# Modulation rows of a spectral and gated-MLP block: four of six parts summed as columns and read back through DRAM

## The chip, the cores and the metric

One core of a Trainium2 chip runs the whole kernel in one launch. The metric is device time in microseconds, the median of several executions. A profile is one more execution, recorded by the hardware: it gives the start and duration of every instruction on TensorE (PE), VectorE (DVE), ScalarE (ACT), GpSimd (POOL) and the DMA queues, of which SyncE (SP) issues most. "Span" is the time from the first to the last recorded instruction.

## What is computed

Cut to what matters here (S = 2048 rows, D = 512, all float32):

```python
mod = (silu(c) @ w_mod).reshape(6, 512)        # c: 512 numbers, w_mod: 512 x 3072
sa, ca, ga, sb, cb, gb = mod                   # parts 0..5, one row of 512 each
h = layernorm(x) * (1 + ca) + sa
a, b = h @ dft_hid_re.T, h @ dft_hid_im.T
x = x + ga * (dft_seq_re @ a - dft_seq_im @ b)
h = layernorm(x) * (1 + cb) + sb
z = gelu(h @ w_in); z1, z2 = z[:, :896], layernorm(z[:, 896:])
x = x + gb * ((z1 * (w_sp @ z2 + b_sp)) @ w_out)
```

The case is about `mod`: six rows of 512 numbers, each a product of the vector silu(c) with a 512 x 512 block of w_mod. Parts 2 to 5 (ga, sb, cb, gb) are wanted as tiles in which all 128 partitions hold the same row, since they multiply or are added to row-major tiles.

## The kernel before

Every large product is made exactly enough by splitting each float32 operand into a high part (rounded, on ScalarE) and a low remainder (a subtraction, on VectorE), and by three matmuls for each tile: high x high, high x low, low x high (`matmul3`, lines 95 to 97).

The first stage, where the change lies, multiplies the sequence-DFT matrices with the normalised rows. It goes in numbered steps n = 0 to 127. A step takes one chunk, 128 x 512, of a DFT matrix: its 32 x 32 blocks are transposed on VectorE from a loaded block (`turn_two`, two chunks at a time, line 227), its high part `ah` is made on ScalarE (`prep_hi`, line 256), its low part `al` on VectorE (`prep_lo`, line 263), and `mm_a` runs 12 matmuls with it, against the high and low parts `hh` and `hl` of row tile s (`hi_h` line 424, `lo_h` line 429). There are four buffers for `ah` and three for `al`. `prep(n)` makes `al` of chunk n+2, then on even n the transposes of chunks n+4 and n+5, then `ah` of chunk n+3.

All the other work of the stage is put between these steps by hand: `at(n, f, ...)` notes that f is called after step n, in the order of the calls to `at`, and `run(n)` calls what was noted. An engine runs its instructions in the order in which they were issued, so these numbers fix the order on every engine, and on the DMA queues of SP and POOL too. In the loop a step is `prep(n)`, `mm_a(n)`, `run(n)`.

Among the work placed so:

- The hidden-DFT matrices are turned, weighted and split into `hth` and `htl` (tags ht0 to ht3, and w0 for a row that comes back through DRAM). For the second matrix this ends at step 49.
- `post_y` and `post_h`, from step 55 on, finish rows of the first half: `post_y` multiplies by mods[2] on VectorE, `post_h` multiplies by mods[4] on VectorE and adds mods[3] on GpSimd. `scale_wo`, much later, multiplies by mods[5].
- Parts 0 and 1 of the modulation are made as columns: the block of w_mod is loaded in a form in which VectorE can turn it into tiles with the output index on the partitions (`load_columns`, `weigh_column`: a transpose at line 176, then a product with the row silu(c) at line 328), and ScalarE's accumulator sums each partition (`sum_column`, line 333). Four such columns of 128 make a part.
- Parts 2 to 5 go another way. `load_mod` loads the block with the input index on the partitions (line 291). `sum_mod` adds the four slices, each scaled by its number of silu(c), on VectorE (one operation at line 302, three at line 304). `split_mod` splits the sum (lines 90 and 91), and `spread_mod` lets TensorE add over the partitions and spread the result, with a matrix of ones (lines 355 and 356, one pair of matmuls for each part); `keep_mod` copies it out of PSUM on ScalarE (line 296).

Of the kernel before, what the change touches and what calls it, by code (L numbers as in the profile page):

```python
# [8 lines left out]
F32 = mybir.dt.float32  # L9
F32R = mybir.dt.float32r  # L10
AF = mybir.ActivationFunctionType
ALU = mybir.AluOpType

P = 128
# [5 lines left out]
def fnet_gmlp_kernel(  # L20
# [32 lines left out]
    nc = tc.nc  # L53
    S, D = x.shape[1:]
# [5 lines left out]
    ND = D // P  # L60
# [5 lines left out]
    def pool(name, side="left", bufs=1):  # L66
        return tc.tile_pool(name=name, bufs=bufs, side=side, reuse_waits="tile")
# [3 lines left out]
    cpool = ctx.enter_context(pool("cpool"))  # L71
# [4 lines left out]
    dram = ctx.enter_context(tc.tile_pool(name="dram", bufs=1, space=bass.MemoryType.DRAM))  # L76
    ctx.enter_context(tc.manual_schedule())

    def bank(k, name):
        return psum.tile([P, 512], F32, tag=f"bank{k}", bufs=1, name=name)  # L80
# [7 lines left out]
    def split(hi, lo, src):  # L88

        nc.scalar.activation(hi, src, AF.Copy)  # L90
        nc.vector.tensor_tensor(lo, src, hi.bitcast(F32), op=ALU.subtract)
# [31 lines left out]
    def at(n, f, *a):  # L123
        fill.setdefault(n, []).append((f, a))
# [50 lines left out]
    def squares(dst, block, k):  # L175
        nc.vector.transpose(dst.rearrange("p (b i) -> p b i", i=32), block[:, :, 32 * k:32 * k + 32])
# [90 lines left out]
    htpool = p2.enter_context(pool("htpool", "right"))  # L267
    rows = p2.enter_context(pool("rows", "right"))
# [6 lines left out]
    hpre = hq.enter_context(pool("hpre"))  # L275

    ccol = cpool.tile([P, ND], F32, name="ccol")
# [4 lines left out]
    sc = cpool.tile([P, ND], F32, name="sc")  # L282
    busy = rows.tile([P, D], F32, tag="row", bufs=6, name="busy")
    nc.vector.memset(busy, 1.0)
    wm, mods = {}, {}

    def load_mod(j):
        w = hpre.tile([P, ND, D], F32, tag="hraw", bufs=1, name=f"wm{j}")
        wm[j] = [w[:, k, :] for k in range(ND)]
        for k in range(ND):  # L290
            nc.sync.dma_start(wm[j][k], w_mod[k * P:(k + 1) * P, j * D:(j + 1) * D])

    def keep_mod(j, ps, pl, plus_one):
        if j not in mods:
            mods[j] = pl.tile([P, D], F32, tag="ht0" if j == 3 else f"mod{j}", bufs=1, name=f"mod{j}")
        nc.scalar.activation(mods[j], ps, AF.Copy, bias=1.0 if plus_one else 0.0)

    def sum_mod(j, ks=range(4)):
        w = wm[j]
        for k in ks:  # L300
            if k == 0:
                nc.vector.tensor_scalar(w[0], w[0], sc[:, 0:1], None, op0=ALU.mult)
            else:
                nc.vector.scalar_tensor_tensor(w[0], w[k], sc[:, k:k + 1], w[0], op0=ALU.mult, op1=ALU.add)

    WB, WT = {}, {}
    COL = {j: cpool.tile([P, ND], F32, name=f"col{j}") for j in range(3)}

    def load_row():

        nc.sync.dma_start(ccol, c.rearrange("b (k p) -> p (b k)", p=P))
        WB["c"] = rows.tile([P, D], F32, tag="row", bufs=6, name="crow")
        nc.sync.dma_start(WB["c"], c[0].partition_broadcast(P))

    def silu_row():
        nc.scalar.activation(sc, ccol, AF.Silu)
        nc.scalar.activation(WB["c"], WB["c"], AF.Silu)

    def load_columns(j):
        pl, tag = (hpre, "hraw") if j else (spool, "wb")  # L320
        WB[j] = pl.tile([P, 16, P], F32, tag=tag, bufs=1, name=f"wb{j}")
        load_block(WB[j], quad(w_mod, 0, j))

    def weigh_column(j, k):
        tag, bufs = ("row", 6) if k % 2 else ("y", 1)
        WT[j, k] = rows.tile([P, D], F32, tag=tag, bufs=bufs, name=f"wt{j}_{k}")
        squares(WT[j, k], WB[j], k)
        nc.vector.tensor_tensor(WT[j, k], WT[j, k], WB["c"], op=ALU.mult)

    def sum_column(j, k):  # L330

        w = WT.pop((j, k))
        nc.scalar.activation(w, w, AF.Copy, accum_out=COL[j][:, k:k + 1])

    def scale_columns():
        col = COL[1]
# [6 lines left out]
        for _ in range(n):  # L343
            nc.tensor.matmul(ps, ones, busy, start=True, stop=True)

    def split_mod(j):
        w = wm[j][0]
        wm[j] = [hpre.tile([P, D], F32R, tag=f"ht{1 + i}", bufs=1, name=f"ws{j}_{i}") for i in range(2)]
        split(*wm[j], w)

    def spread_mod(j, k, pl, plus_one):

        ps = bank(k, f"modp{j}")
        hi, lo = wm.pop(j)
        nc.tensor.matmul(ps, ones_r, hi, start=True, stop=False)
        nc.tensor.matmul(ps, ones_r, lo, start=False, stop=True)
        keep_mod(j, ps, pl, plus_one)

    X, XG, LN, NRM, h_hi, h_lo = {}, {}, {}, {}, {}, {}

# [605 lines left out]
    for n, *todo in ((0, (turn_one, 3), (prep_hi, 3), (stats_first, 2), (prep_lo, 3), (turn_one, 4), (prep_hi, 4)),  # L966
                     (1, (norm_first, 2), (hi_h, 2), (prep_lo, 4), (lo_h, 2), (turn_one, 5), (prep_hi, 5)),
                     (2, (stats_first, 3), (prep_lo, 5), (turn_one, 6), (prep_hi, 6)),
                     (3, (norm_first, 3), (hi_h, 3), (prep_lo, 6), (lo_h, 3), (turn_one, 7), (prep_hi, 7), (ones_x, 4), (stats_x, 4)),
                     (4, (ones_x, 5), (ones_x, 6), (prep_lo, 7), (turn_two, 8), (stats_x, 5), (prep_hi, 8), (norm_x, 4), (hi_h, 4), (stats_x, 6)),  # L970
                     (5, (ones_x, 7), (prep_lo, 8), (lo_h, 4), (prep_hi, 9), (norm_x, 5), (hi_h, 5)),
                     (6, (prep_lo, 9), (turn_two, 10), (lo_h, 5), (norm_x, 6), (hi_h, 6), (stats_x, 7)),
                     (7, (norm_x, 7)), (8, (lo_h, 6), (hi_h, 7)), (9, (lo_h, 7))):
        for f, *a in todo:
            at(n, f, *a)
    at(0, load_x, 1, range(2, 4))
    at(2, load_row)
    at(9, silu_row)
    at(4, load_x, 2)
    at(5, load_columns, 1)  # L980
# [4 lines left out]
    for s, n in ((8, 10), (9, 10)):  # L985
        m = n + (s == 9)
# [10 lines left out]
    for j, ns in ((1, (13, 15, 17, 18)), (0, (21, 22, 23, 24))):  # L997
        for k, n in enumerate(ns):
            at(n, weigh_column, j, k)
            at(n + 1, sum_column, j, k)  # L1000
# [6 lines left out]
    ones_r = htpool.tile([P, P], F32R, name="ones_r")  # L1007
    at(24, nc.scalar.activation, ones_r, ones, AF.Copy)
    at(26, change_pools)
    for j, turn, weigh, row, fold, hi in ((0, (25, 26, 27, 28), (29, 29, 30, 30), 26, (34, 34, 35, 36), (38, 35, 36, 37)),  # L1010
# [8 lines left out]
        n = weigh[3] + (3 if j == 0 else 1)  # L1019
# [3 lines left out]
        for k in (1, 2, 3, 0):  # L1023
            at(hi[k], make_ht, j, k)
            at(hi[k] + 1, make_ht_lo, j, k)
    for j, load_at, n, m, k, plus_one in ((2, 41, 49, 50, 7, False), (4, 52, 56, 58, 7, True),
                                          (3, 60, 65, 66, 7, False), (5, 68, 79, 80, 6, False)):
        at(load_at, load_mod, j)
        at(n, sum_mod, j, [0, 1])
        at(m, sum_mod, j, [2, 3])  # L1030
        at(m + 1, split_mod, j)
        at(m + 3, spread_mod, j, k, cpool if j == 5 else htpool, plus_one)
    for t in range(NQ):
        n = 8 * NQ * (t + 1)
        for i in range(4):
            y = N2 - 1 if t == NQ - 1 else (54, 56, 58, 60)[i] if t == 0 else n + (7, 9, 11, 13)[i] if t == 1 else n + 1 + 3 * i
# [32 lines left out]
    w0 = ctx.enter_context(ExitStack())  # L1069
# [14 lines left out]
    for i, u in enumerate((r, g, b) for g in range(2) for b in range(4) for r in range(2)):  # L1084
        n = 85 + 5 * i if i < 8 else N2 + (13, 15, 28, 29, 31, 33, 35, 37)[i - 8]
        m = n + (4 if i < 8 or i > 9 else (9, 13)[i - 8])
# [31 lines left out]
    for i, p in enumerate(PROD):  # L1118
        for k in range(8):
            n = NB[p] + 2 * k  # L1120
# [39 lines left out]
    for f in range(NF):  # L1160
        n = NB[6] + 3 * f
# [66 lines left out]
```

## Time and profile before

| | us |
|---|---|
| median of 3 runs | 946.18 (946.17 to 946.81) |
| the profiled execution | 946.31 |
| its span | 944.5 |
| VectorE: the 16 operations of `sum_mod` | 0.48 each at line 302, 0.75 each at line 304 |
| ScalarE: a copy out of PSUM (`keep_mod`) | 0.60 |
| loads of w_mod for parts 2 to 5 (16 of 256 KB) | 4.7 from issue to landing |

Page rows name a source line, an engine, an operation and the tiles as out<-in. A duration of TensorE is that of one matmul from its start to its modelled end, and matmuls overlap; the distance of two starts is what one costs in a row without gaps. "Idle" in square brackets is the time that the engine sat before an instruction, with what ended it. The granted clock of TensorE is full throughout.

### The profile page before, as it was taken

What the parts mean: (1) busy time and instruction counts of PE and PEld (TensorE: products, weight loads), DVE (VectorE), ACT (ScalarE), POOL (GpSimd) and SP (SyncE); (2) the same over time, 40 slices, a digit from 0 to 9 for tenths busy, and PEclk for the clock granted to TensorE, in tenths of its full rate; (3) what the DMA queues carried; (4) which work ended last, traced back from release to release, by engine and by line L of the source; (5) the groups of instructions that cost most, each with busy time, mean ns of one, the idle gap of its engine ahead of it and who ended that gap; (6) DMA issues with size and microseconds to landing.
All of it is one profiled execution on the core that took longest, in us unless ns stands there. A gap on an engine that the chain in (4) does not pass through costs nothing.

```text
span 944.5 us, 12279 instructions
## 1 busy us (share of the span) xinstructions
PE 937.9 (99%) x4160; PEld 781.1 (83%) x4160; DVE 705.7 (75%) x1045; ACT 386.2 (41%) x663; POOL 171.3 (18%) x327
## 2 busy tenths in 40 slices
PE   8999999999999999999999999999999999999998
PEld 6888888888888888888888999888888888888886
DVE  7799857775576657767978587877788688885872
ACT  3695424232232222322876356553544444331221
POOL 1430000221621145123332265200000000000000
PEclk9999999999999999999999999999999999999999
DMA  9997554576528965996398985555554456733551
GB/s 198 245 226 152 110 129 99 148 177 156 145 78 204 278 202 154 284 275 146 93 339 288 321 269 164 148 112 135 123 134 90 108 116 142 205 104 119 170 183 59
DMA packets 251406, 161.25 MB, mean 171 GB/s; under 512 B 134416, under 2 KB 220688, under 8 KB 251216
## 3 DMA queue, kind: packets, MB, share of 16 engines
q1 hardware_dynamic: 237008, 120.62, 52.5%
q0 software_dynamic: 11984, 39.07, 11.4%
q10 hardware_dynamic: 2352, 0.79, 0.3%
q8 instruction: 32, 0.52, 0.3%
q14 instruction: 30, 0.25, 0.1%
HBM read 123.73 MB, written 36.70 MB: 170 GB/s over the span
## 4 chain that ended last, share of the span: by engine, by line
PE 96%; DMA 1%; SPq 1%; DVE 0%; issue 0%; POOL 0%; ACT 0%; ACTq 0%; DVEq 0%
PE gp L97 11%; PE gp L96 11%; PE gp L95 11%; PE gw L95 10%; PE gw L96 10%; PE gw L97 10%; PE yp L97 3%; PE yp L96 3%; PE yp L95 3%; PE z2p L96 3%; PE z2p L95 3%; PE z2p L97 3%; PE op L97 3%; PE op L95 3%; PE op L96 3%; PE z1p L96 1%
## 5 line engine op out<-in xcount | busy, mean ns | idle before, releaser
L256 ACT ACTIVATE ah<-t 128x512 fp32r<-128x512 f32 x263 | 164.5, 627 | 312.6 <-PE gp L97 181.3
L263 DVE TENSOR_TENSOR al<-t,ah 128x512 fp32r<-128x512 f32 x264 | 180.3, 686 | 137.6 <-PE gp L96 61.6
L97 PE MATMUL gp<-ah,hl 128*128 128x512 f32 x480 | 186.9, 389 | 0.3 <-DVE hl L429 0.3
L95 PE MATMUL gp<-ah,hh 128*128 128x512 f32 x480 | 186.7, 389 | 0.0
L96 PE MATMUL gp<-al,hh 128*128 128x512 f32 x480 | 186.7, 389 | 0.0
L97 PE MATMUL gw<-ah,bl 128*128 128x512 f32 x400 | 155.6, 389 | 0.0
L96 PE MATMUL gw<-al,bh 128*128 128x512 f32 x400 | 155.6, 389 | 0.0
L95 PE MATMUL gw<-ah,bh 128*128 128x512 f32 x400 | 155.6, 389 | 0.0
L97 PEld LDWEIGHTS gp<-ah,hl 128*128 128x128 f32 x480 | 90.1, 188 | 19.3 <-DVE hl L429 0.7
L96 PEld LDWEIGHTS gp<-al,hh 128*128 128x128 f32 x480 | 90.1, 188 | 18.8
L95 PEld LDWEIGHTS gp<-ah,hh 128*128 128x128 f32 x480 | 90.1, 188 | 18.8
L97 PEld LDWEIGHTS gw<-ah,bl 128*128 128x128 f32 x400 | 75.1, 188 | 15.7
L95 PEld LDWEIGHTS gw<-ah,bh 128*128 128x128 f32 x400 | 75.1, 188 | 15.5
L96 PEld LDWEIGHTS gw<-al,bh 128*128 128x128 f32 x400 | 75.1, 188 | 15.5
L227 DVE STREAM_TRANSPOSE t<-stage 128x1024 f32<-128x1024 f32 x62 | 76.8, 1239 | 5.5 <-DMA stage<-in_A_dft_seq_re_dram 5.5
L221 DVE STREAM_TRANSPOSE t<-stage 128x1024 f32<-128x1024 f32 x56 | 69.4, 1240 | 0.1
L772 ACT ACTIVATE bh<-z 128x512 fp32r<-128x512 f32 (+1 forms) x56 | 32.8, 586 | 66.1 <-PE gw L96 66.1
L750 POOL DMA_DIRECT2D s_d<-sj x64 | 35.1, 550 | 105.5 <-DVE sj L742 79.3
L95 PE MATMUL yp<-hth,gh 128*128 128x512 f32 x128 | 49.8, 389 | 0.0
L96 PE MATMUL yp<-htl,gh 128*128 128x512 f32 x128 | 49.8, 389 | 0.0
L97 PE MATMUL yp<-hth,gl 128*128 128x512 f32 x128 | 49.8, 389 | 0.0
L96 PE MATMUL z2p<-wil,ah 128*128 128x448 f32 x128 | 46.7, 365 | 0.0
(206 smaller groups left out, 1439.4 us busy)
## 6 DMA issues: line engine op xcount, KB each, us to landing
sj<-in_B_w_sp_dram SPq DMA_DIRECT2D x32, 512.0 KB, 8.4
s_d<-sj POOLq DMA_DIRECT2D x64, 256.0 KB, 4.3
stage<-s_d SPq DMA_DIRECT2D x128, 128.0 KB, 2.8
stage<-in_A_dft_seq_re_dram SPq DMA_DIRECT2D x60, 256.0 KB, 5.3
stage<-in_A_dft_seq_im_dram SPq DMA_DIRECT2D x60, 256.0 KB, 5.4
stage<-in_B_w_sp_dram SPq DMA_DIRECT2D x96, 128.0 KB, 3.2
stage<-h_d SPq DMA_DIRECT2D x32, 256.0 KB, 7.0
wm<-in_w_mod_dram SPq DMA_DIRECT2D x16, 256.0 KB, 4.7
```

Of the source, the lines that this page charges most:

```text
L95: nc.tensor.matmul(acc, ah, bh, start=first, stop=False, skip_group_check=go_on)
L96: nc.tensor.matmul(acc, ah, bl, start=False, stop=False, skip_group_check=go_on)
L97: nc.tensor.matmul(acc, al, bh, start=False, stop=last, skip_group_check=go_on)
L221: nc.vector.transpose(t.rearrange("p r (b i) -> p r b i", i=32), st[:, :, :, 16 * k:16 * k + 32])
L227: nc.vector.transpose(t.rearrange("p k (b i) -> p k b i", i=32), st[:, :, 32 * k:32 * k + 64].rearrange("p b (k i) -> p k b i", k=2))
L256: nc.scalar.activation(AH[n], source(n), AF.Copy)
L263: nc.vector.tensor_tensor(AL[n], source(n), AH[n].bitcast(F32), op=ALU.subtract)
L750: nc.gpsimd.dma_start(s_d[m, r, g][b * P:(b + 1) * P, :], a)
L772: nc.scalar.activation(BH[p, k][:, :w], b_of(p, k), AF.Copy)
```

## The change

Parts 2 to 5 are made as parts 0 and 1 were: transposed and multiplied on VectorE, four columns to a part, and summed by ScalarE's accumulator into a column of 128 numbers. GpSimd then stores each column into a row of 512 numbers in DRAM (`store_mod`, for part 4 after adding 1), and `read_mod` reads the row back into all 128 partitions. `load_mod`, `sum_mod`, `split_mod`, `spread_mod` and `keep_mod` go, with their eight matmuls, and so do the column load of c and its silu. The columns use the buffers of tags w0 and ht1 to ht3, which the hidden-DFT work has left. The columns of a part are spread over the steps given in the table at the end. Apart from that, `lo_h` of row 6 moves from step 8 to step 7.

```diff
-        nc.sync.dma_start(ccol, c.rearrange("b (k p) -> p (b k)", p=P))
-        WB["c"] = rows.tile([P, D], F32, tag="row", bufs=6, name="crow")
+        WB["c"] = cpool.tile([P, D], F32, tag="mod5", bufs=1, name="crow")
         nc.sync.dma_start(WB["c"], c[0].partition_broadcast(P))
...
-        nc.scalar.activation(sc, ccol, AF.Silu)
         nc.scalar.activation(WB["c"], WB["c"], AF.Silu)
+
+    mod_d = [dram.tile([1, D], F32, name=f"mod_d{j}") for j in range(6)]
...
     def weigh_column(j, k):
-        tag, bufs = ("row", 6) if k % 2 else ("y", 1)
-        WT[j, k] = rows.tile([P, D], F32, tag=tag, bufs=bufs, name=f"wt{j}_{k}")
+        if j > 1:
+            WT[j, k] = hpre.tile([P, D], F32, tag=("w0", "ht1", "ht2", "ht3")[k], bufs=1, name=f"wt{j}_{k}")
+        else:
+            tag, bufs = ("row", 6) if k % 2 else ("y", 1)
+            WT[j, k] = rows.tile([P, D], F32, tag=tag, bufs=bufs, name=f"wt{j}_{k}")
...
         w = WT.pop((j, k))
-        nc.scalar.activation(w, w, AF.Copy, accum_out=COL[j][:, k:k + 1])
+        nc.scalar.activation(w, w, AF.Copy, accum_out=COL[j if j < 2 else j % 2][:, k:k + 1])
...
+    def store_mod(j, k, plus_one):
+
+        col = COL[j % 2][:, k:k + 1]
+        if plus_one:
+            nc.gpsimd.tensor_scalar(col, col, 1.0, 1.0, op0=ALU.add, op1=ALU.mult)
+        nc.gpsimd.dma_start(mod_d[j][0].rearrange("(a k i) -> k a i", a=4, i=32)[k], col)
+
+    def read_mod(j, pl):
+        mods[j] = pl.tile([P, D], F32, tag="ht0" if j == 3 else f"mod{j}", bufs=1, name=f"mod{j}")
+        nc.gpsimd.dma_start(mods[j], mod_d[j][0].partition_broadcast(P))
...
-                     (7, (norm_x, 7)), (8, (lo_h, 6), (hi_h, 7)), (9, (lo_h, 7))):
+                     (7, (lo_h, 6), (norm_x, 7)), (8, (hi_h, 7)), (9, (lo_h, 7))):
...
-    for j, load_at, n, m, k, plus_one in ((2, 41, 49, 50, 7, False), (4, 52, 56, 58, 7, True),
-                                          (3, 60, 65, 66, 7, False), (5, 68, 79, 80, 6, False)):
-        at(load_at, load_mod, j)
-        at(n, sum_mod, j, [0, 1])
-        at(m, sum_mod, j, [2, 3])
-        at(m + 1, split_mod, j)
-        at(m + 3, spread_mod, j, k, cpool if j == 5 else htpool, plus_one)
+    for j, load_at, ns in ((2, 41, (48, 48, 49, 50)), (4, 51, (54, 56, 58, 60)),
+                           (3, 61, (64, 65, 66, 67)), (5, 68, (73, 75, 77, 79))):
+        at(load_at, load_columns, j)
+        for k, n in enumerate(ns):
+            at(n, weigh_column, j, k)
+            at(n + 1, sum_column, j, k)
+            at(n + 1, store_mod, j, k, j == 4)
+        at(ns[-1] + 2, read_mod, j, cpool if j == 5 else htpool)
```

How the order on VectorE moves at steps 48 to 51, where part 2 is made. A row is line, operation, out<-in and shape; `al` are the low parts of chunks 51, 52 and 53, `t` the transposes of chunks 54 and 55, `htl` the hidden-DFT low parts, `wm` and `ws` the old sum and its split, `wt` the columns, `wb` the loaded block, `crow` the row silu(c). Before:

```order
L520 TENSOR_TENSOR htl_2_1612<-ht_2_1336,hth_2_1588 128x512
L263 TENSOR_TENSOR al_1618<-t_1527,ah_1594 128x512
L520 TENSOR_TENSOR htl_3_1634<-ht_3_1357,hth_3_1614 128x512
L520 TENSOR_TENSOR htl_0_1636<-ht_0_1191,hth_0_1616 128x512
L302 TENSOR_SCALAR wm_1377<-wm_1377,sc 128x512
L304 SCALAR_TENSOR_TENSOR wm_1377<-wm_1377,sc 128x512
L263 TENSOR_TENSOR al_1640<-t_1592,ah_1620 128x512
L227 STREAM_TRANSPOSE t_1642<-stage_1399 128x1024
L304 SCALAR_TENSOR_TENSOR wm_1377<-wm_1377,sc 128x512 x2
L263 TENSOR_TENSOR al_1667<-t_1592,ah_1649 128x512
L91 TENSOR_TENSOR ws_1_1684<-wm_1377,ws_0_1683 128x512
```

In the changed kernel, from two rows further on (line numbers are those of the new file, where 502 is the old 520):

```order
L176 STREAM_TRANSPOSE wt_1_1625<-wb_1381 128x512
L312 TENSOR_TENSOR wt_1_1625<-wt_1_1625,crow 128x512
L263 TENSOR_TENSOR al_1628<-t_1531,ah_1598 128x512
L502 TENSOR_TENSOR htl_3_1644<-ht_3_1361,hth_3_1618 128x512
L502 TENSOR_TENSOR htl_0_1646<-ht_0_1195,hth_0_1620 128x512
L176 STREAM_TRANSPOSE wt_2_1652<-wb_1381 128x512
L312 TENSOR_TENSOR wt_2_1652<-wt_2_1652,crow 128x512
L263 TENSOR_TENSOR al_1655<-t_1596,ah_1630 128x512
L227 STREAM_TRANSPOSE t_1657<-stage_1403 128x1024
L176 STREAM_TRANSPOSE wt_3_1680<-wb_1381 128x512
L312 TENSOR_TENSOR wt_3_1680<-wt_3_1680,crow 128x512
L263 TENSOR_TENSOR al_1685<-t_1596,ah_1664 128x512
```

Between `htl_2` and `al` of chunk 51 stand now two columns, `wt_0` (not shown, the same two operations) and `wt_1`; one column stands ahead of `al` of chunk 52 and one ahead of `al` of chunk 53, in place of the sums. The subtraction for `ws` behind `al` of chunk 53 is gone.

The order on GpSimd's queue in the same place, of the changed kernel, from step 49 on. `mod_d` is the row in DRAM, `col` the columns, `mod` the tile that is read, `xr` rows of x for `post_y`, and the last three are the norm of the first finished row:

```order
L335 DMA mod_d_132<-col_127 4x32x1 x3
L507 DMA xr_0_1683<-in_A_x_dram 128x512
L335 DMA mod_d_132<-col_127 4x32x1
L339 DMA mod_1726<-mod_d_132 128x512
L507 DMA xr_1_1728<-in_A_x_dram 128x512
L334 TENSOR_SCALAR col_127<-col_127 128x1
L335 DMA mod_d_134<-col_127 4x32x1
L533 DMA x_d_76<-xr_0_1683 128x512
L107 TENSOR_SCALAR mvy<-mvy 128x1
L108 TENSOR_TENSOR rsy<-mvy,mhalf 128x1
L115 TENSOR_SCALAR nmry<-mvy,rsy 128x1
```

Before, the two loads of `xr`, the store of `x_d` and the norm stood there one behind the other; now the first load stands behind three column stores, and the second behind the read of part 2, which waits for its four stores.

On VectorE at steps 7 and 8, of the changed kernel: `hl_485` is row 6's low part, `al_488` that of chunk 10, `t_490` the transposes of chunks 12 and 13.

```order
L103 BN_STATS bstx<-x_174 128x6
L105 BN_AGGR mvx<-bstx 128x2
L411 TENSOR_TENSOR hl_485<-xn_374,hh_460 128x512
L263 TENSOR_TENSOR al_488<-t_450,ah_471 128x512
L227 STREAM_TRANSPOSE t_490<-stage_342 128x1024
L263 TENSOR_TENSOR al_513<-t_450,ah_492 128x512
L411 TENSOR_TENSOR hl_529<-xn_420,hh_506 128x512
```

Before, `hl` of row 6 stood two rows lower, behind the transposes of chunks 12 and 13 and ahead of `al` of chunk 11.

More of the change, by code (lines that the diff above doesn't have):

```diff
@@ L284, in fnet_gmlp_kernel @@
     nc.vector.memset(busy, 1.0)
[L285 to L304, printed above, removed]
+    mods = {}
     WB, WT = {}, {}
@@ L344, in keep_busy @@
             nc.tensor.matmul(ps, ones, busy, start=True, stop=True)
[L346 to L357, printed above, removed]
+    def store_mod(j, k, plus_one):
[6 more added lines that the diff above has]
+        nc.gpsimd.dma_start(mods[j], mod_d[j][0].partition_broadcast(P))
     X, XG, LN, NRM, h_hi, h_lo = {}, {}, {}, {}, {}, {}
```

## The prediction, made before the changed kernel ran

> **What bounds the kernel now.** I read the page first, then the waits of TensorE alone, then the timelines of the places that the change touches.
>
> ```profile
> span 944.5 us, 12279 instructions
> PE 937.9 (99%) x4160; PEld 781.1 (83%) x4160; DVE 705.7 (75%) x1045; ACT 386.2 (41%) x663; POOL 171.3 (18%) x327
> ```
> ```profile
> PE busyp L344 <- DVE busy L284: 1.5, 1, 1.5
> PE gp L449 <- DVE ah L940: 1.4, 1, 1.4
> PE gp L97 <- DVE hl L429: 0.3, 1, 0.3
> ```
>
> The second fence is the whole list of TensorE's waits (us in total, times, longest): two at the start, and one of 0.3 us on row 6's hl. In all the rest TensorE goes from matmul to matmul. So a matmul less is time less, and nothing else counts unless it makes TensorE wait. The profiled execution took 946.31 us, 1.8 us around its span of 944.5; the median of the runs shown is 946.18. I sum against 946.31 and take off 0.13 at the end.
>
> **Eight matmuls go.** Rows are start, duration.
>
> ```profile
> 167.47 0.39 PE L355 MATMUL modp<-ws,ones_r 128*128 128x512 f32 x1
> 167.69 0.39 PE L356 MATMUL modp<-ws,ones_r 128*128 128x512 f32 x1
> 167.92 0.39 PE L95 MATMUL gp<-ah,hh 128*128 128x512 f32 x1
> ```
>
> The duration of 0.39 us is no price: the next matmul starts before it is over. The price is the distance of the starts, 167.92 - 167.47 = 0.45 us for a pair, 0.227 for one (944.5 / 4160 is the same). Four pairs: **-1.82 us**, not 8 x 0.39 = 3.1. The pair stood behind no wait, so nothing else goes with it; TensorE now reaches the next chunk 0.45 us earlier each time, and every deadline of the other engines with it.
>
> **Row 6's hl.** TensorE, then VectorE (DVE) and ScalarE (ACT), at chunk 10:
>
> ```profile
> 35.63 0.39 PE L96 MATMUL gp<-al,hh 128*128 128x512 f32 x1
> 36.30 0.50 PE L97 MATMUL gp<-ah,hl 128*128 128x512 f32 x1 [0.28 <-DVE hl L429]
> 36.63 0.40 PE L95 MATMUL gp<-ah,hh 128*128 128x512 f32 x1
> ```
> ```profile
> 33.83 0.69 DVE L263 TENSOR_TENSOR al<-t,ah 128x512 fp32r<-128x512 f32 x1 [0.54 <-ACT ah L256]
> 34.44 1.24 DVE L227 STREAM_TRANSPOSE t<-stage 128x1024 f32<-128x1024 f32 x1
> 35.60 0.65 DVE L429 TENSOR_TENSOR hl<-xn,hh 128x512 fp32r<-128x512 f32 x1
> ```
> ```profile
> 32.64 0.63 ACT L424 ACTIVATE hh<-xn 128x512 fp32r<-128x512 f32 x1
> ```
>
> From 35.63 to 36.63 lie 1.00 us, where two matmuls take 0.45: the stall costs 0.55, more than the 0.28 that the waits name, because the first matmul behind it takes long too. After the change hl stands ahead of al and the transposes. Its input hh is done at 33.27, inside the 0.54 us in which VectorE waited anyway, so hl runs from about 33.3 to 34.0, al from 33.9 to 34.6, and the transposes are done near 35.75 as before. TensorE needs al at 35.63 and hl at 35.86; neither is late: **-0.55 us**. What could take this back is the next thing that TensorE meets, now 0.55 us earlier; one wait of VectorE there has a releaser that TensorE does not move:
>
> ```profile
> 46.65 1.25 DVE L227 STREAM_TRANSPOSE t<-stage 128x1024 f32<-128x1024 f32 x1 [4.47 <-DMA stage<-in_A_dft_seq_re_dram]
> ```
>
> TensorE did not wait there before (it is not on the list), so between 0 and 0.55 come back; I take 0, since the load starts earlier too when chunk 12's block is worked off earlier.
>
> **The columns on VectorE.** A part cost VectorE one TENSOR_SCALAR, three SCALAR_TENSOR_TENSOR and one subtraction; it now costs four transposes and four products. The same pair of operations runs already for parts 0 and 1:
>
> ```profile
> 48.98 0.70 DVE L176 STREAM_TRANSPOSE wt<-wb 128x512 f32<-128x512 f32 x1
> 49.72 0.69 DVE L328 TENSOR_TENSOR wt<-wt,crow 128x512 f32<-128x512 f32 x1
> 50.33 0.68 DVE L263 TENSOR_TENSOR al<-t,ah 128x512 fp32r<-128x512 f32 x1
> ```
>
> One column is 50.33 - 48.98 = 1.35 us. VectorE's room, by stretch (from:to, length, then busy time of PE, PEld, DVE, ACT, POOL); the stretches hold part 2, part 3 and the end of part 5:
>
> ```profile
> 149.30:167.90 18.60, 18.60 (x83) 15.39 (x82) 16.44 (x24) 8.29 (x15) 0.00 (x0) 1.00 0.42 91
> 203.00:220.00 17.00, 17.00 (x76) 14.08 (x76) 13.28 (x18) 7.24 (x12) 0.90 (x2) 1.00 0.75 161
> 270.00:286.00 16.00, 16.00 (x72) 13.25 (x71) 14.31 (x19) 7.50 (x13) 3.19 (x4) 1.00 0.20 59
> ```
>
> Part 3 adds 4 x 1.35 = 5.4 and removes about 3.6, into 3.7 us of idle: fits. Part 5 has three of its columns in earlier chunks, so its dense end gets lighter. Part 2 is the tight one: 2.2 us idle, most of it ahead of the columns. There the deadlines have to be followed one by one. VectorE before, and then TensorE's first use of al of chunks 51, 52 and 53:
>
> ```profile
> 156.18 0.68 DVE L263 TENSOR_TENSOR al<-t,ah 128x512 fp32r<-128x512 f32 x1
> 156.78 1.29 DVE L520 TENSOR_TENSOR htl<-ht,hth 128x512 fp32r<-128x512 f32 x2
> 157.98 0.48 DVE L302 TENSOR_SCALAR wm<-wm,sc 128x512 f32<-128x512 f32 x1
> 158.50 0.75 DVE L304 SCALAR_TENSOR_TENSOR wm<-wm,sc 128x512 f32<-128x512 f32 x1
> 159.17 0.69 DVE L263 TENSOR_TENSOR al<-t,ah 128x512 fp32r<-128x512 f32 x1
> ...
> 160.93 1.50 DVE L304 SCALAR_TENSOR_TENSOR wm<-wm,sc 128x512 f32<-128x512 f32 x2
> 162.35 0.69 DVE L263 TENSOR_TENSOR al<-t,ah 128x512 fp32r<-128x512 f32 x1
> ```
> ```profile
> 159.53 0.39 PE L96 MATMUL gp<-al,hh 128*128 128x512 f32 x1
> ...
> 162.25 0.39 PE L96 MATMUL gp<-al,hh 128*128 128x512 f32 x1
> ...
> 164.97 0.39 PE L96 MATMUL gp<-al,hh 128*128 128x512 f32 x1
> ```
>
> al of 51 (start 156.18) now has two columns ahead of it: 156.18 + 2.70 = 158.88, done 159.56, wanted 159.53: just late. al of 52: a column (1.35) in place of 157.98 to 159.17 (1.19): 159.17 + 2.70 + 0.16 = 162.03, done 162.72, wanted 162.25: 0.5 late. al of 53: a column in place of 160.93 to 162.35 (1.42): 162.35 + 2.86 - 0.07 = 165.14, done 165.83, wanted 164.97: **0.9 late**. These are distances from one schedule, so they don't add: TensorE ends this stretch 0.9 us behind. The subtraction of part 2 (0.69) then goes and chunk 54 is in time. VectorE's chain here hangs on TensorE through freed al buffers, so the earlier 0.55 changes nothing in it. Each of the three stalls may cost a slow first matmul (0.1 in the hl stall), but an early one only eats into the next lateness: 0 to 0.1 more. I take **+0.9**; below it is bounded by 0, if columns ran some 0.3 us shorter each, which no row shows.
>
> **The sums on ScalarE, the stores and reads.** A sum is one ACTIVATE:
>
> ```profile
> L333 ACT ACTIVATE wt<-wt x8: 613/617/634, 52.7 to 78.9; 128x512 f32<-128x512 f32 x8
> ```
>
> Sixteen come, eight activations (split and copy) go. ScalarE is busy 8.29 of 18.60 us in the tightest stretch, and it makes ah three chunks (8 us) ahead: cost 0; without that cover a sum is 0.6. The sum waits for its product, and the ah behind it with it; in part 2 the ah of chunk 53 follows the second sum, so near 160.3, with TensorE there at 164.7.
>
> GpSimd's (POOL's) queue now has the column stores, each waiting for a sum, and the read, waiting until all four have landed; behind it stand a load of xr and the small operations of the next row's norm. No row shows a store in 4-byte pieces of this kind; the neighbours (KB each, median us to landing):
>
> ```profile
> wb<-in_w_mod_dram SPq DMA_DIRECT2D x8, 256.0 KB, 8.3
> w<-hrow_d POOLq DMA_DIRECT2D x2, 256.0 KB, 5.5
> hrow_d<-w0r POOLq DMA_DIRECT2D x2, 2.0 KB, 2.1
> ccol<-in_c_dram SPq DMA_DIRECT2D x1, 2.0 KB, 6.2
> ```
>
> hrow_d is a store of one contiguous row, ccol a load of 512 pieces of 4 bytes; a column store has 128. I bound it by 2.1 and 6.2 and take 2.1, the store. The last sum of part 2 ends near 166.0, its store is out by 166.6, landed 168.7 to 172.8, the read out half a microsecond later and landed (5.5) near 174.8 to 178.9. First use:
>
> ```profile
> 174.29 0.69 DVE L549 TENSOR_TENSOR y<-y,mod 128x512 f32<-128x512 f32 x1
> ...
> 176.57 0.67 DVE L263 TENSOR_TENSOR al<-t,ah 128x512 fp32r<-128x512 f32 x1
> ```
> ```profile
> 184.47 0.39 PE L96 MATMUL gp<-al,hh 128*128 128x512 f32 x1
> ```
>
> VectorE may wait 0 to 4.5 us at 174.3, and al of chunk 58 (176.57) behind it, which TensorE wants 184.47 - 177.24 = 7.2 us after it was done: hidden, cost 0. The same cover takes a late block for part 4 (its load starts near 164.5, once part 2's last transpose has freed the buffer, and 8.3 lands it at 173). Parts 4, 3 and 5 are stored many chunks ahead of their use or, for part 3, wanted by GpSimd's sum alone. On SP, four issues replace four, and ccol's goes.
>
> A rule speaks against these stores. The Trainium skill, "DMA: Bandwidth & Descriptors", section "Rules for kernel authors", says that a last dimension that isn't contiguous becomes one descriptor for each element and should be rearranged. By it the store would lie near ccol's 6.2, not hrow_d's 2.1. Nothing in the sum changes; it bears on the slower rival below. No run here shows such a store yet.
>
> **Sum.** 946.31 - 1.82 - 0.55 + 0.9 = 944.84, less 0.13 is 944.7; with half of the possible 0.1 behind the stalls, **944.8 us**, 0.15% faster. A measurement of this kernel can tell about 0.2% (1.9 us) from no change, so this counts as the same.
>
> **Rivals.** (1) The cover holds at part 2, and no al is late: 946.18 - 2.37 = 943.8, 0.25% faster. For it: eight such columns ran between 49 and 79 us, among denser work, without a wait of TensorE. Against it: the three deadlines, of which the last is missed by 0.9. (2) Part of the gain at row 6 is given back at the load near 46.65, or the stalls restart badly: 0.3 to 1.5 more, 945.1 to 946.3. For it: TensorE arrives earlier at a transfer that doesn't. Against it: it did not wait there. (3) Slower: part 2 comes back too late through DRAM. VectorE then stands at y, al of chunk 58 comes late, and TensorE waits. Store and read took 7.6 us by the rows taken, and the 7.2 us of cover are used up when they take about 14.3. To end 0.2% slower (948.1) TensorE has to lose 3.3 more than forecast, so 17.6 us for the two. Against it: the longest neighbours are 6.2 and 5.5, 11.7 together. (4) That the change doesn't do what it says: the order of TensorE shows the eight matmuls gone, so not here.
>
> **How the numbers follow.** Forecast (944.5 to 945.1) 0.55; rival 1 (943.5 to 944.2) 0.27; rival 2 0.12; rival 3 0.06. The range reaches from rival 1's 943.6 to 946.0, most of rival 2, and leaves out rival 3 and the edges. Faster by over 0.2% (below 944.3): rival 1 and a little of the forecast, 0.32; slower 0.06; within 0.2% the rest, 0.62.
>
> **What would show it.** Right: 4152 matmuls; no wait on hl at chunk 10; in TensorE's waits an entry on al from VectorE's line 263 near 157 to 164 us, 0.7 to 1.0 in total; no such wait near 205 to 285. Wrong: no wait on al there (rival 1), a longer one, a wait of TensorE near 46 to 50, or one near 180 with VectorE waiting for the read of mod 2 behind it.

## The result, and the profile after

| | before | changed |
|---|---|---|
| median, measured together | 946.55 us (6 runs) | 968.54 us (6 runs, 967.15 to 972.82) |
| ratio | | 1.0236 [1.0213, 1.0258] |
| profiled execution, span | 946.31, 944.5 | 968.28, 966.5 |

The forecast was 944.8 us. The kernel is 2.4% slower, far outside the range, on the side that was given 0.06.

The page of the changed kernel: span, the engines' busy time, and the granted clock of TensorE in 40 slices of 24.2 us.

```profile
span 966.5 us, 12344 instructions
PE 946.9 (98%) x4152; PEld 784.4 (81%) x4152; DVE 714.2 (74%) x1057; ACT 389.4 (40%) x686; POOL 186.4 (19%) x351
PEclk9999999998999999999989999999999999999999
```

The eight matmuls are gone (4152). Two slices show 8 in the clock, the ones from 217 to 242 and from 483 to 507 us. All of TensorE's waits (us in total, times, longest):

```profile
PE gp L96 <- DVE al L263: 7.2, 4, 3.3
PE z1g L95 <- ACT z1k L659: 4.8, 1, 4.8
PE gp L95 <- DVE gl L91: 2.5, 2, 2.2
PE busyp L328 <- DVE busy L284: 1.5, 1, 1.5
```

The wait on hl is gone. New are four on al, two on gl (the low parts of the stage's results, made on VectorE), and one of 4.8 us on `z1k`, a tile of the second stage which the diff does not touch. TensorE's timeline at three places:

```profile
186.66 0.50 PE L96 MATMUL gp<-al,hh 128*128 128x512 f32 x1 [3.33 <-DVE al L263]
186.99 0.39 PE L97 MATMUL gp<-ah,hl 128*128 128x512 f32 x1
...
189.12 0.63 PE L95 MATMUL gp<-ah,hh 128*128 128x512 f32 x1
189.55 0.63 PE L96 MATMUL gp<-al,hh 128*128 128x512 f32 x1
...
191.86 0.50 PE L96 MATMUL gp<-al,hh 128*128 128x512 f32 x1 [0.83 <-DVE al L263]
...
215.71 0.50 PE L96 MATMUL gp<-al,hh 128*128 128x512 f32 x1 [1.79 <-DVE al L263]
...
219.34 0.79 PE L95 MATMUL gp<-ah,hh 128*128 128x512 f32 x1 [2.21 <-DVE gl L91]
219.93 0.63 PE L96 MATMUL gp<-al,hh 128*128 128x512 f32 x1
...
482.20 0.79 PE L95 MATMUL z1g<-ah,w 128*128 128x512 f32 x1 [4.79 <-ACT z1k L659]
482.79 0.63 PE L96 MATMUL z1g<-al,w 128*128 128x512 f32 x1
483.22 0.63 PE L97 MATMUL z1g<-ah,w 128*128 128x512 f32 x1
```

Read the distances of the starts. Behind some of the stalls they are 0.43 us (189.12 to 189.55, 482.79 to 483.22) in place of 0.227, for a while. So a stall can cost more than its wait. Summed over every pair of starts, what lies above 0.227 us apiece gives the whole difference:

| place (us) | lost beyond 0.227 a matmul | the wait ahead |
|---|---|---|
| 36 | -0.55 (gone) | hl |
| 50 | +1.6 | al, behind transposes that wait for a load |
| 160 to 167 | +0.9 | al of chunks 51 to 53 |
| 182 to 193 | +6.1 | al, 3.3 and 0.8 |
| 213 to 226 | +7.4 | al 1.8, gl 2.2 |
| 288 | +0.6 | gl |
| 477 to 489 | +7.9 | z1k 4.8 |
| eight matmuls | -1.8 | |
| sum | +22.1 (span: +22.0) | |

What stands behind the place at 182 to 193 is VectorE (DVE) at the same time, then SP's queue, then GpSimd's (start, duration, and in brackets what the engine waited for):

```profile
184.56 0.71 DVE L176 STREAM_TRANSPOSE wt<-wb 128x512 f32<-128x512 f32 x1 [13.33 <-DMA wb<-in_w_mod_dram]
185.92 0.68 DVE L263 TENSOR_TENSOR al<-t,ah 128x512 fp32r<-128x512 f32 x1
188.85 0.69 DVE L531 TENSOR_TENSOR y<-y,mod 128x512 f32<-128x512 f32 x1 [1.65 <-DMA mod<-mod_d]
191.13 0.67 DVE L263 TENSOR_TENSOR al<-t,ah 128x512 fp32r<-128x512 f32 x1
213.42 0.69 DVE L532 TENSOR_TENSOR xr<-y,xr 128x512 f32<-128x512 f32 x1 [2.88 <-DMA xr<-in_A_x_dram]
```
```profile
166.75 9.68 SPq L154 DMA_DIRECT2D wb<-in_w_mod_dram  x4
176.53 6.85 SPq L154 DMA_DIRECT2D stage<-in_A_dft_seq_re_dram  x4
```
```profile
167.15 0.70 POOL L335 DMA_DIRECT2D mod_d<-col  x1 [1.79 <-ACT wt L317]
180.52 0.60 POOL L339 DMA_DIRECT2D mod<-mod_d  x1 [12.67 <-DMA mod_d<-col]
```

Part 2's last column is stored at 167.15. The read could only go at 180.52, since a store lands in 4.1 to 15.9 us (the tile view of `mod_d`, below). VectorE's longer wait is on the block of **part 4**: its four issues on SP began at 166.75, right beside those stores, took 9.68 us to go out, and the first transpose waited 13.33 us. The al at 185.92, of chunk 57, stood behind it, and TensorE wanted it at 183.2: that is the first stall.

The read sets the second. VectorE's first product with it began at 188.85, the al at 191.13, of chunk 58, stood behind that, and TensorE went on at 191.86. Without the first stall it would have been there 12 matmuls of 0.227 us after 183.2, at 185.9. So by this reckoning the late read alone would have cost 6.0 of the 6.1 us lost here, and a block that came in time would have saved almost nothing.

At 213 to 219 it is a load of xr. GpSimd could issue it only at 205.10, once the store of x_d from 197.23 had landed (7.9 us; 2.3 in the median in the kernel before), and VectorE could use it at 213.42, 8.3 us later (4.5 in the median before). The row's norm on GpSimd follows it, ScalarE waits for the norm, and its copies for gh and VectorE's gl come behind:

```profile
216.75 0.81 ACT L119 ACTIVATE h<-xr,nmry,rsy 128x512 f32<-128x512 f32 x1 [6.75 <-POOL nmry L115]
```

The tile views of `mod_d` and, second, of `wb` say from issue to landing (us, least, median, longest):

```profile
DMA to landing us min/median/max: 4.1/8.5/15.9
```
```profile
DMA to landing us min/median/max: 3.3/9.2/17.6
```

### The profile page after: what moved, and what is told of

The parts are those of the page before. It is cut to its first block, busy times and chain, and to the rows that moved or that the text cites. A ratio compares the mean times of both kernels' runs of the same rounds, so it can differ in the third digit from the quotient of the medians.

```text
span 966.5 us, 12344 instructions
## 1 busy us (share of the span) xinstructions
PE 946.9 (98%) x4152; PEld 784.4 (81%) x4152; DVE 714.2 (74%) x1057; ACT 389.4 (40%) x686; POOL 186.4 (19%) x351
## 4 chain that ended last, share of the span: by engine, by line
PE 85%; DMA 6%; issue 3%; DVE 3%; POOL 1%; SPq 1%; ACT 1%; ACTq 0%; DVEq 0%; POOLq 0%
PE gw L95 9%; PE gw L97 9%; PE gw L96 9%; PE gp L95 9%; PE gp L96 9%; PE gp L97 9%; PE z2p L96 3%; PE z2p L95 3%; PE z2p L97 3%; PE op L97 3%; PE yp L97 3%; PE op L95 3%; PE yp L96 3%; PE yp L95 3%; PE op L96 3%
## 5 line engine op out<-in xcount | busy, mean ns | idle before, releaser
L96 PE MATMUL gp<-al,hh 128*128 128x512 f32 x480 | 189.2, 394 | 7.4 <-DVE al L263 7.2
L95 PE MATMUL gp<-ah,hh 128*128 128x512 f32 x480 | 188.9, 394 | 2.5 <-DVE gl L91 2.5
```

The source lines that it names most:

```text
L95: nc.tensor.matmul(acc, ah, bh, start=first, stop=False, skip_group_check=go_on)
L96: nc.tensor.matmul(acc, ah, bl, start=False, stop=False, skip_group_check=go_on)
```

## The experiments

Two causes seemed at work: one at 482 us, where no modulation is made, and one at 165 to 290 us. The theory for the first: taking `crow` out of the ring of six row buffers shifts every later allocation in that ring by one, so other data lies at each address when the next stage lays its own tiles over the ring. For the second: the column stores in 4-byte pieces land late and hold up the loads beside them. Rivals for the second: the loads themselves (in runs of 512 bytes, now 24 of them in place of 8), or the read and its place in GpSimd's queue.

### The ring set back in step

The changed kernel, with one allocation more in the ring.

```diff
         WB["c"] = cpool.tile([P, D], F32, tag="mod5", bufs=1, name="crow")
+        spare = rows.tile([P, D], F32, tag="row", bufs=6, name="spare")
+        nc.gpsimd.memset(spare[:, 0:1], 0.0)
```

> The changed kernel with one more allocation of tag row where the tile crow left that ring of six buffers (one element of it is written); nothing else differs. Theory ring: the wait of 5.2 us at 482 us (and the slow clock behind it, some 8 us in all) comes from the ring being one buffer out of step, so that a buffer of the second stage lies over the row whose store lands last; the wait goes and the time falls by about 8 us, to 960. Rival: the store is late because DMA is late as a whole; then the wait stays and the time stays near 968.

Measured: 958.25 us, ratio 1.0120 [1.0104, 1.0137]; 10.3 less than the changed kernel (measured apart; the profiled spans differ by 10.4). The wait on `z1k` has left the list, and the rest of it stands:

```profile
PE gp L96 <- DVE al L263: 6.4, 4, 3.0
PE gp L95 <- DVE gl L91: 4.1, 2, 2.2
```

Of the 10.3, 7.9 are the place at 482 us. The rest comes from 213 to 226 us, where two stalls of 1.2 and 2.6 us from start to start were this time not followed by matmuls at 0.43 (3.6 lost in place of 7.4); a stall near 285 us was 1.6 longer in return. Crow stayed where the change put it; a memset and a buffer that nobody reads removed the stall, so it is the position in the ring and not crow's new address.

### No stores at all

From the former, with the column stores left out and the reads fetching other rows, so that no read waits for a store.

```diff
-        nc.gpsimd.dma_start(mod_d[j][0].rearrange("(a k i) -> k a i", a=4, i=32)[k], col)
...
-        nc.gpsimd.dma_start(mods[j], mod_d[j][0].partition_broadcast(P))
+        nc.gpsimd.dma_start(mods[j], w_mod[0, j * D:(j + 1) * D].partition_broadcast(P))
```

> The same ring, and no column is stored: the four reads fetch a row of w_mod instead, so the modulation rows of parts 2 to 5 are other numbers (the sums are still made). Theory stores: the column stores in pieces of 4 bytes hold up every DMA engine, so without them the load for part 4 lands within 9 us instead of 17.6, the waits of TensorE near 186 and 216 us go, and the time falls to about 946 (the stall of 0.9 us near 160 stays). Rival loads: the loads of w_mod in runs of 512 bytes are what holds up DMA; then the waits at 186 and 216 stay, at about 958 to 960. Rival read: a read through GpSimd's queue is late by itself; then part of the stall near 188 stays.

Measured: 946.35 us, ratio 0.9989 [0.9979, 0.9998]; 11.9 less. TensorE's waits behind the first 10 us, and VectorE and SP at part 4's block:

```profile
PE gp L96 <- DVE al L263: 1.2, 1, 1.2
```
```profile
177.56 0.71 DVE L176 STREAM_TRANSPOSE wt<-wb 128x512 f32<-128x512 f32 x1 [6.36 <-DMA wb<-in_w_mod_dram]
```
```profile
166.73 4.04 SPq L154 DMA_DIRECT2D wb<-in_w_mod_dram  x4
```

VectorE waits for the block even here, 6.36 us, and TensorE does not. In the changed kernel the issues take 9.68 in place of 4.04 us, the wait is 13.33, and TensorE stands 3.5 of it (183.2 to 186.66): the cover at this place is about 10 us.

### The loads in long runs, the stores kept

From the ring kernel, parts 2 to 5 loaded in runs of 2048 bytes as before the change.

```diff
+        if j > 1:
+            w = WB[j].rearrange("p b i -> p (b i)")
+            for k in range(ND):
+                nc.sync.dma_start(w[:, k * D:(k + 1) * D], w_mod[k * P:(k + 1) * P, j * D:(j + 1) * D])
+            return
```

> The same ring, with the stores, but the loads of parts 2 to 5 in runs of 2048 bytes, as before the change (the columns are then sums of other numbers, at the same cost). Theory stores: nothing gets better, the column stores still land in 8 to 16 us and the time is near 960. Rival loads: the waits near 186 and 216 us go, near 946.

Measured: 959.89 us, ratio 1.0133 [1.0118, 1.0148]. Blocks still land in 2.8 to 18.4 us and stores in 3.9 to 16.4. The shape of the loads is not the cause.

### The same bytes in pieces of 128

From the ring kernel: the four sums of a part go into one 128 x 32 tile, VectorE turns it (0.2 us), and four stores carry the row out in runs of 32 numbers.

```diff
-        nc.gpsimd.dma_start(mod_d[j][0].rearrange("(a k i) -> k a i", a=4, i=32)[k], col)
+        if k < 3:
+            return
+        nc.vector.transpose(PC[1], PC[0])
...
+        for a in range(4):
+            nc.gpsimd.dma_start(mod_d[j][0].rearrange("(a k i) -> a k i", a=4, i=32)[a], PC[1][32 * a:32 * a + 4, :])
```

> The same ring, loads as in the change; the four sums of a part go into one 128x32 tile, one small transpose on VectorE brings them into runs of 128 bytes, and four stores of four such runs go out in place of four stores of 128 pieces of 4 bytes. Theory stores, by size of the piece: stores land within 3 us, the waits near 186 and 216 us go, near 946. Rival: any store and read through DRAM at this place is late, whatever its pieces; near 958.

Measured: 947.51 us, ratio 1.0002 [0.9992, 1.0011], 10.7 less than with 4-byte pieces. Tile views of `mod_d` and `wb`, issue to landing:

```profile
DMA to landing us min/median/max: 1.5/6.2/7.4
```
```profile
DMA to landing us min/median/max: 3.4/7.1/9.4
```

Still sixteen stores of 512 bytes on the same queue (all four of a part now go behind its last sum), but the longest lands in 7.4 us and the longest block load in 9.4 instead of 19.6. The expectation of stores within 3 us was too low, but the time falls all the same: the 4-byte pieces carry the second cause. What is left over in the profile (of an execution of 948.88 us, the longest of the ten) is 0.9 us at 160 to 167, a stall of 1.2 at 50 us, one of 0.95 at 209 and one of 1.6 at 457 us.

### Parts of the change put into the kernel before

Three kernels, each the one before with one thing added: row 6's hl at step 7; crow out of the ring; sixteen column stores of 4-byte pieces at the change's steps, which nothing reads.

```diff
-                     (7, (norm_x, 7)), (8, (lo_h, 6), (hi_h, 7)), (9, (lo_h, 7))):
+                     (7, (lo_h, 6), (norm_x, 7)), (8, (hi_h, 7)), (9, (lo_h, 7))):
```

> The kernel before with one edit of the change: row 6's hl at step 7. Theory hl: the wait of 0.3 us at 36 us goes and the span falls by 0.55. If the stall of 1.5 us at 50 us (the transposes of chunk 16, waiting for their load), which every variant of the change shows, comes from this edit, it stands here too and the span rises by about 1; if it comes from the missing load of c by columns, it isn't here.

```diff
-        WB["c"] = rows.tile([P, D], F32, tag="row", bufs=6, name="crow")
+        WB["c"] = cpool.tile([P, D], F32, tag="mod5", bufs=1, name="crow")
```

> The kernel before with one edit of the change: the tile crow leaves the ring of row buffers and takes the place that mods[5] gets later. Nothing else moves. Theory ring: ScalarE's copies of z1g wait for the store of a finished row near 461 us, TensorE stands about 5 us there and runs slowly behind it: 952 to 955. Rival: the shift of the ring costs only where DMA is late already; then no change, 946.2 to 947.5.

```diff
+    def store_col(j, k):
+        nc.scalar.activation(COL[0][:, k:k + 1], sc[:, k:k + 1], AF.Copy)
+        nc.gpsimd.dma_start(mod_d[j][0].rearrange("(a k i) -> k a i", a=4, i=32)[k], COL[0][:, k:k + 1])
...
+    for j, ns in ((2, (48, 48, 49, 50)), (4, (54, 56, 58, 60)), (3, (64, 65, 66, 67)), (5, (73, 75, 77, 79))):
+        for k, n in enumerate(ns):
+            at(n + 1, store_col, j, k)
```

> The kernel before with 16 column stores added, in pieces of 4 bytes, at the steps where the change has them, each behind a small copy on ScalarE that fixes its time; nothing reads them and nothing else moves. Theory stores: they alone make the transfers around them late: packets of 512 bytes that take microseconds, the loads of wm and stage landing in 10 us and more near 166 us, and stalls of TensorE where those loads have little room, 947 to 956. Rival: stores hurt only because a read waits for them; then all landings stay as before and the time within 0.3 us of before.

| added to the kernel before | us | ratio |
|---|---|---|
| hl of row 6 | 947.60 | 1.0004 [0.9994, 1.0013] |
| crow out of the ring | 953.61 | 1.0068 [1.0053, 1.0083] |
| sixteen stores | 948.38 | 1.0009 [1.0000, 1.0019] |

**Crow** alone costs 6.4 us. TensorE's wait, and ScalarE's row behind it (in the kernel before, the same three activations at 461.25 wait for nothing):

```profile
PE z1g L95 <- ACT z1k L677: 4.5, 1, 4.5
```
```profile
468.06 1.57 ACT L677 ACTIVATE z1k<-z1g 128x512 f32<-128x512 f32 x3 [5.87 <-DMA h_d<-h]
```

`h` is a tile of the row ring, and `z1k` lies in a pool that is opened once the ring's pool is closed. With the ring shifted, the buffer that `z1k` gets is one whose last content still has to be stored to `h_d`.

**hl** takes its wait away, and no gain is measured: +0.4 us, with an interval from -0.6 to +1.2, whose end just holds the 0.55 forecast. TensorE's first matmul with chunk 15's al in the kernel with hl moved, and then in the one with only crow moved, where the hl stall stands as before:

```profile
50.64 0.50 PE L96 MATMUL gp<-al,hh 128*128 128x512 f32 x1 [1.44 <-DVE al L263]
```
```profile
50.65 0.50 PE L96 MATMUL gp<-al,hh 128*128 128x512 f32 x1 [0.55 <-DVE al L263]
```

The same moment, with and without the 0.55 us: both are set by a load of the DFT matrix, for which VectorE waits ahead of the transposes at 48.77 in both kernels. In these two traces the gain is given back there.

**The stores** alone land as late as in the changed kernel (4.2 to 18.0 us, tile view of `mod_d`), and the loads of w_mod beside them in 2.9 to 19.2 us, where the kernel before has 4.7 in the median. Yet the time grows by 1.2 us only. TensorE has one new stall, at 210 us, and it is again behind a late load of xr (VectorE waits 3.87 us for it at 204.64); nothing is lost at 182 to 193, where no read waits here. Late transfers alone do not make the 11 us.

### The column load of c put back

From the kernel with 128-byte pieces: whether the vanished load of c is what makes the stall at 50 us.

```diff
         nc.sync.dma_start(WB["c"], c[0].partition_broadcast(P))
+        nc.sync.dma_start(ccol, c.rearrange("b (k p) -> p (b k)", p=P))
```

> The packed stores of r4_packed, with the column load of c put back ahead of crow's (nothing uses it). Theory ccol: this load happened to space the loads of the start, and with it the stall at 50 us goes: 1 to 1.5 us less than r4_packed, near 946.3 against 947.5. Rival: the stall stays, since it comes from the hl edit or from anything that moves the start; no change.

Measured: 947.93 us, ratio 1.0008 [0.9998, 1.0017]; the stall at 50 us stays (1.56). It is not from c.

### Part 2 earlier

If lateness costs only where nothing covers it, then room helps. Part 2's columns go to steps 43 to 46, in a row buffer that is free there, and part 4's load to step 47; once with 128-byte pieces, once with the change's 4-byte pieces.

```diff
-    for j, load_at, ns in ((2, 41, (48, 48, 49, 50)), (4, 51, (54, 56, 58, 60)),
+    for j, load_at, ns in ((2, 41, (43, 44, 45, 46)), (4, 47, (54, 56, 58, 60)),
...
+        if j == 2:
+            WT[j, k] = rows.tile([P, D], F32, tag="y", bufs=1, name=f"wt{j}_{k}")
```

> r4_packed with part 2's columns at steps 43 to 46 (in the buffer y, which is free then) in place of 48 to 50, and the load for part 4 at step 47 in place of 51. Theory columns: VectorE has room there, so the three stalls near 160 to 167 us (0.9 us) go, the load for part 4 lands before its transposes, and with it the stall on gl near 209 us goes; what is left is the eight matmuls less: 1.8 us below the kernel before, less what the stall near 50 us costs on this chip, so a ratio of 0.997 to 0.999. Rival: the stall at 160 comes from something else in that place (the second matrix's parts); then it stays and the time is that of r4_packed.

> The same early steps, but the column stores in pieces of 4 bytes again. Theory stores: each store still holds up the transfers beside it, so the landings stay at 8 us and more and stalls near 190 and 215 remain, though the early load of part 4 takes the first one away: 949 to 955. Rival: the stores hurt only because part 4's load came right behind them; then the time is that of f1_early.

| part 2 early, ring in step | us | ratio |
|---|---|---|
| pieces of 128 bytes | 945.27 (11 runs; before 947.30, 21 runs) | 0.9979 [0.9970, 0.9988] |
| pieces of 4 bytes | 945.93 (10 runs) | 0.9987 [0.9978, 0.9997] |

The expectation for the second missed by a wide margin: the stores still land late, in 3.9 to 17.7 us, and GpSimd's read of a part still waits for them, but the read of part 2 goes out at 165.41 in place of 180.52, and beyond the place at 50 us TensorE loses only 1.1 us, at 273, on a late gl. That is nearly what the rival said. Two things moved here, part 2's columns and the load for part 4, and no run takes them apart; by the reckoning above it is the earlier read that counts. GpSimd's queue with 4-byte pieces:

```profile
165.41 0.61 POOL L343 DMA_DIRECT2D mod<-mod_d  x1 [10.67 <-DMA mod_d<-col]
237.19 0.59 POOL L343 DMA_DIRECT2D mod<-mod_d  x1 [17.58 <-DMA mod_d<-col]
```

TensorE's waits with 128-byte pieces; the stalls at 160 to 167 and at 209 are gone, and 0.9 is the place at 50 us:

```profile
PE busyp L334 <- DVE busy L284: 1.5, 1, 1.5
PE gp L96 <- DVE al L263: 0.9, 1, 0.9
PE gp L440 <- DVE ah L931: 0.6, 1, 0.6
```

The kernel with 128-byte pieces and part 2 early beats both kernels, before and changed: 0.21% below the one before, with its whole interval below, and 2.4% below the changed one (945.27 to 968.54, measured apart). The two are not told apart from each other (their intervals overlap).

## Why the prediction was wrong, point by point

- **Eight matmuls, -1.82**: right. 4152 stand in the page, and in places without a stall the distance is still 0.227.
- **The columns of part 2 on VectorE, +0.9**: right, in mechanism and size. TensorE lost 0.9 us between 160 and 167 us, at the first matmul with al of chunks 51, 52 and 53. Reckoned from one schedule, as the prediction did, these came 0.08, 0.45 and 0.78 us late (forecast: just late, 0.5 and 0.9), and the last slow restart adds 0.11. Each delay is too short to stand in the list of waits, where the prediction looked for it; the starts show it. Moving these columns to steps 43 to 46 took it away.
- **Sums on ScalarE, 0**: nothing in TensorE's waits names them.
- **Row 6's hl, -0.55**: the wait went, and in the traces the gain went with it at the load near 50 us, the place that the second rival names. "I take 0" for what comes back, on the ground that the load starts earlier too, was the wrong end there: the whole 0.55 came back. The stall there is longer than that (1.6 in the changed kernel), but the kernel with only crow moved has 0.8 of it without this edit, since the load itself came later. The transposes behind it ran at 46.65 in the profile of the kernel before, at 48.7 in the changed kernel, and at 48.8 and 48.1 with crow alone and with the stores alone. The last adds nothing to the engines' orders before 155 us, so the early load at 46.65 may belong to that one execution rather than to its kernel.
- **The stores and reads, "I take 2.1, the store", "hidden, cost 0"**: this step failed, and it cost about 11 us (958.25 to 947.51 once the pieces are long). The stores landed in 4.1 to 15.9 us, median 8.5. The Trainium skill's rule that the prediction cites, "DMA: Bandwidth & Descriptors", section "Rules for kernel authors", gives one descriptor for each element and no time; the row nearest to it, the column load's 6.2, was the better guide, and the measured median lies above that, too. The "longest neighbours 6.2 and 5.5" bounded a transfer by others of its size, in place of leaving the upper end open for a form that no row showed. For part 2 it was 13.4 us from the issue of the last store to that of the read (167.15 to 180.52) and 8.3 from there to its first use (188.85), 21.7 together where the sum had 7.6.
- **The third rival** (chance 0.06) had the mechanism: VectorE stands at y, al of chunk 58 comes late, TensorE waits. Its condition, 17.6 us for the store and the read, was met with 21.7; by its own sum 21.7 - 14.3 = 7.4 us would be lost at this place, and 6.1 were. What it did not have is what the stores do to other transfers.
- **"The same cover takes a late block for part 4"**, with the load at 8.3 us: the load's time was taken from a kernel that has no such stores beside it. Blocks landed up to 17.6 us after their issue, the cover ran out, and al of chunk 57 came late ahead of 58. That there was a cover was right: without stores VectorE waited 6.36 us there at no cost. The loads of xr, late at 213 to 219, stand in no term, and "no such wait near 205 to 285" did not hold.
- **Not in the sum at all: the ring.** The prediction has no word on the diff's line that takes crow from `rows` to `cpool`, and the section on the change does not name it beside the move of `lo_h`. It shifts a ring of six for the rest of the program: 6.4 us alone, 7.9 in the changed kernel, at 477 us, some 175 us after the change's last instruction, the read of part 5 at 301.
- **The range** is said to reach from rival 1's 943.6; the sum for that rival is 943.8. Nothing hangs on it.

Without the ring and the stores, -1.82 + 0.9 with nothing for hl is -0.9, and the kernel without stores is 0.96 below the kernel before (946.35 to 947.31). That the two figures meet so closely is in part luck: the profiled spans of both kernels are 944.5, since the one without stores loses 1.5 us at 50 where the profile of the kernel before has no stall. The later runs of the kernel before took about 947.2 where its profiled execution took 946.31, and no trace shows where.

Shown by runs: the ring (taken alone and undone), the size of the pieces, that the loads' shape and c have no part, that the damage goes when part 2 and the load for part 4 come earlier. Reckoned and not taken alone: that the late read makes the stall at 182 to 193. Open: how a store of 4-byte pieces holds up the transfers of other queues, and why the load for the transposes near 46.65 came some 2 us later in the other kernels.

## What to carry to other kernels

Moving one allocation out of a rotating set of buffers moves every later one, so look at who overlays that set afterwards, and keep the count when nothing else matters. Price a transfer of a form that the trace does not show with an open upper end, and price what it does to the transfers beside it; a column that must go to DRAM is first turned on chip so that it leaves in long pieces. A stall of some microseconds can cost more than its wait, since matmuls may run at half rate behind it; so place work with a late input where the cover is larger than the worst landing, not the median.

## What the runs showed of the hardware that was not expected

- **Matmuls at half rate behind a stall.** After 5.18 us without a start (477.02 to 482.20) the next matmuls started 0.427 us apart until about 488.3; after the two stalls at 215.71 and 219.34 until 225.5; after the one at 186.66 six at full rate came first and then six at 0.427. A single gap of 2.5 us, in the kernel before with the stores added, had none. Three places cost 21.4 us with waits of only 13 us. The windows view of the changed kernel (from:to, length, busy time of PE, PEld, DVE, ACT and POOL, granted clock, DMA share, GB/s) shows it as the granted clock, 0.86, 0.77 and 0.69:

```profile
183.00:195.00 12.00, 7.85 (x28) 5.56 (x27) 8.62 (x14) 3.27 (x8) 2.86 (x6) 0.86 0.67 150
213.00:228.00 15.00, 11.01 (x35) 8.17 (x34) 12.85 (x19) 6.40 (x13) 3.31 (x6) 0.77 0.93 167
481.00:492.00 11.00, 9.80 (x30) 7.81 (x31) 4.34 (x5) 7.78 (x15) 0.61 (x2) 0.69 0.46 97
```

  What decides it can be read from the same view. In all twelve traces the granted clock changes only at the ends of intervals of 3.413 us that follow each other without a gap (in the changed kernel at 188.00, 191.42, 218.72, 225.55, 481.55 and 488.37). Until a kernel's last matmul it was halved eight times, in four of the kernels, each time behind an interval in which TensorE was busy for 1.44 us at most, and never behind one with 1.55 us or more. Two such intervals and the half rate behind the first, of the changed kernel, and then the one of the single gap, of the kernel before with the stores added:

```profile
184.59:188.00 3.41, 1.34 (x6) 1.13 (x7) 2.58 (x4) 1.25 (x3) 0.84 (x2) 1.00 1.17 275
188.00:191.41 3.41, 3.03 (x8) 1.83 (x6) 2.46 (x5) 0.00 (x0) 0.74 (x3) 0.50 0.42 58
215.31:218.72 3.41, 1.43 (x5) 0.86 (x5) 2.19 (x4) 1.97 (x4) 1.22 (x3) 1.00 1.21 246
```
```profile
206.89:210.30 3.41, 1.55 (x7) 0.94 (x5) 2.18 (x3) 2.32 (x5) 0.87 (x3) 1.00 0.35 64
```

  So how a stall lies on these intervals matters as much as its length. The kernel with the ring set back had gaps of 1.23 and 2.58 us at 213 to 218, but 2.14 and 1.66 us of matmuls in the two intervals there, and kept the full rate.

  The Trainium skill, "TensorE: Matmul & The Clock Gate", section "Part 1: The HAM clock gate (the "warmup" mystery)", says that the array's clock is halved after an idle window of about 3.4 us that runs freely, and gives 426.7 ns between cold matmuls of 512 columns. The distance agrees with the 0.427 here, and the length with the 3.413 us; but the interval need not be idle here, as the 1.34 and 1.43 us of matmuls above show.
- **A store of 512 bytes in 4-byte pieces delays other queues.** With it 256 KB loads of w_mod land up to 17.6 to 19.7 us after their issue, and up to 9.4 with the same bytes in 128-byte pieces. SP needs 9.68 us to issue four of them for part 4, 4.04 without stores and 3.72 with 128-byte pieces.
- **A restart of TensorE at full clock costs 0.11 us**: the first matmul behind a stall is 0.50 long, and the next starts 0.33 us after it in place of 0.227 (186.66 to 186.99).
